# Sorted attention pairs: a two-row cluster code for the masks, a PSUM copy on ScalarE, and other points for ranks and masks

## The chip, the cores and the metric

The kernel runs on one core of a Trainium2 chip. The metric is the device time of one execution in microseconds (us); the time of a version is the median of several executions. Engines: PE (TensorE), DVE (VectorE), ACT (ScalarE), POOL (GpSimd) and SP (the queue that issues most DMAs). Each engine works through its own instructions in program order.

## The reference

Two parts, one after the other. First, routed attention for 4 batches x 8 heads, 768 tokens, head size 64: every query and every key goes to the nearest of its head's 16 centroids (argmax of the scores with the normalised centroids), and a query attends only to keys of its own cluster. Then a feed-forward layer on the 3072 x 512 result with the activation hardswish:

```python
mask = q_assign[:, :, :, None] == k_assign[:, :, None, :]
scores = np.where(mask, scale * np.matmul(q, k.transpose(0, 1, 3, 2)), -1e9)
x = softmax(scores) @ v               # (B, H, S, D) -> (B*S, H*D)
h = x @ w_in                          # 512 -> 2048
out = (h * np.clip(h + 3, 0, 6) / 6) @ w_out
```

## The kernel before, in words

Heads are worked on in 16 **pairs** of two heads. The first eight pairs take a dense way (768 x 768 scores with an additive mask, until about 250 us). The last eight, pairs 8 to 15, take a **sorted** way: queries and keys are sorted by cluster in DRAM, so that only a band of three 128-wide blocks around the diagonal has to be computed. All of the sorted work is issued by a loop of **rounds** g = 6 to 16, and a round has twelve **points**, 0 to 11 (`points`). A round works on three pairs at once: it computes the band of pair g (now), gets pair g+1 ready (next) and ranks pair g+2 (soon). Before the change the points are:

- 0 to 3: `band_scores` and `band_values` of pair g; point 0 also loads the natural rows of pair g+2 (`load_natural`)
- 4: `band_sums`, and `turn_back` of pair g-1
- 5: `band_divide` of pair g: transposes of the denominators and of the six numerator blocks on PE (L1047, L1051), then on DVE a reciprocal (L1055) and two multiplications that read the PSUM tile `ps` (L1058, tile `xr`); the result is stored by SP (L1064)
- 6: `gather` of pair g (twelve indirect DMAs on POOL), then `turn_natural` of pair g+2: twelve transposes on PE in two halves (L859: q, then k), each copied out by ACT (L860)
- 7: `cluster_scores` of pair g+2
- 8: `load_ranked` of pair g+1 and `load_rows` of pair g+2 (twelve DMAs on SP), then `own_clusters` of pair g+2: three transposes on PE (L878) and twelve small DVE operations in a row, from `mx` (L880) to the last `upto` (L889)
- 9: `order` of pair g+2: PE reads `upto` (L915, L928), DVE makes `edges` and `pos` (L929 to L940)
- 10: `scatter` of pair g+2: 24 indirect DMAs on POOL
- 11: `turn_ranked` and `band_masks` of pair g+1

After the work of each point the loop takes **one item of the feed-forward part** from a list (`fill`). A block of 256 tokens has 15 items: 8 **up items** (0 to 7), then 7 **down items** of which each is 16 matmuls. The items run straight through the rounds: round 6 begins with down item 1 of the first block, and each round takes twelve, so the item at point 5 of rounds 8 to 13 is down 0, up 5, up 2, down 6, down 3 and down 0. 51 items are left when the rounds end (785 us) and run alone.

An up item (`halved`) uses a seven-product scheme: 12 matmuls into PSUM tile `uX`, 16 into `uY`. DVE copies one of the uX blocks to SBUF (L652), adds twice (L645), and after uY adds three times; then ACT applies the ramp (`lift`, L499), and DVE finishes the *previous* item (`clip`, L502, and in every second item four `gated_sums`, L624, on DVE during the rounds). uX and uY, and X and Y of the down items, share a ring of two PSUM buffers (`psum_m`). The weights' sums `tx` come from DRAM: an item issues the load for the item two later (L548) on SP, into a ring of three.

`band_scores`, `turn_back`, `band_divide`, `turn_natural` and `turn_ranked` all take their PSUM tile `ps` from another ring of **two** (`psum_s`): every third user waits until the first one's tile has been read. `open_late` sets up the sorted part once, between the dense part and round 6; its first instruction on POOL is an iota into `places` (L795).

`band_masks` writes the additive mask of a pair as a product over cluster rows: two DVE operations for the query side (L974, L977) and two for the key side (L980, L981), each over 128 x 768.

Of the kernel before, what the change touches and what calls it, by code (L numbers as in the profile page):

```python
# [8 lines left out]
F32 = mybir.dt.float32  # L9
# [110 lines left out]
def fast_path(ctx, tc, ok, q, k, v, centroids, moe_w_in, moe_w_out, out):  # L120
# [457 lines left out]
    def ffn_items(b):  # L578
# [47 lines left out]
        def halved(b, m, u, i, g):  # L626
            token_sums(b, m)
            tx = st.pop(("tx", u))
            xb, xs = st["xb", b, m], st["xs", b, m]
            X = psum_m.tile([P, 4, P], F32, name="uX", tag="m")  # L630

            def part(dst, w, x):
                for kt in range(HK):
                    nc.tensor.matmul(  # L634
                        dst, lhsT=w[:, kt], rhs=x(kt), start=(kt == 0), stop=(kt == HK - 1)
                    )

            def a(s, r):
                return lambda kt: xb[:, s * HK + kt, r * P : (r + 1) * P]

            def s(k):
                return lambda kt: xs[:, k, kt]

            def add(out_, in0, in1):
                nc.vector.tensor_tensor(out=out_, in0=in0, in1=in1, op=ALU.add)  # L645


            part(X[:, 0], tx[:, 1], s(1))
            part(X[:, 1], wi(0, 0, i), a(0, 0))
            part(X[:, 2], wi(0, 1, i), a(0, 1))  # L650
            sx = sxp.tile([P, 4, P], F32, name="sx")
            nc.vector.tensor_copy(out=sx[:, 1], in_=X[:, 1])  # L652
            add(sx[:, 0], X[:, 0], sx[:, 1])
            add(sx[:, 2], X[:, 2], sx[:, 0])
            Y = psum_m.tile([P, 4, P], F32, name="uY", tag="m")
            part(Y[:, 0], tx[:, 0], s(0))
            part(Y[:, 1], wi(1, 0, i), a(1, 0))
            part(Y[:, 2], tx[:, 2], a(1, 1))
            part(Y[:, 3], wi(1, 1, i), s(2))
            add(sx[:, 3], Y[:, 0], sx[:, 0])  # L660
            add(g[:, 3], Y[:, 0], sx[:, 2])
            add(g[:, 0:3], Y[:, 1:4], sx[:, 1:4])
            lift(sx, g)
            finish()
            ending.append(lambda: (clip(g, sx, g), gated_sums(i)))
# [119 lines left out]
    def open_late():  # L785
        whole.close()
        late = ctx.enter_context(ExitStack())
        for name, bufs in (
            ("piecep", 2), ("svp", 1), ("fromp", 1), ("natp", 1), ("sortp", 1), ("bandp", 5),
            ("rowp", 3), ("rankp", 1), ("posp", 4),  # L790
        ):
            st[name] = right(late, name, bufs)
        rankp = st["rankp"]
        st["places"] = rankp.tile([P, S], mybir.dt.int16, name="places")
        nc.gpsimd.iota(  # L795
            st["places"], pattern=[[1, S]], base=0, channel_multiplier=0, allow_small_or_imprecise_dtypes=True
        )
        st["before"] = rankp.tile([P, P], BF16, name="before")
        nc.gpsimd.memset(st["before"], 0.0)
        nc.gpsimd.affine_select(  # L800
            out=st["before"], in_=st["before"], compare_op=ALU.is_ge, fill=1.0, base=0,
            pattern=[[-1, P]], channel_multiplier=1,
        )
        st["every"] = rankp.tile([P, P], BF16, name="every")
        nc.gpsimd.memset(st["every"], 1.0)
        st["runs"] = rankp.tile([P, 2, NCH, 2, C], BF16, name="runs")
        nc.gpsimd.memset(st["runs"], 0.0)
        st["steps"] = rankp.tile([P, 3, 2, 2, C // 2 + C], BF16, name="steps")
        nc.gpsimd.memset(st["steps"], 0.0)
        st["upto"] = rankp.tile([P, 2, C // 2 + 2 * D], BF16, name="upto")  # L810
        nc.gpsimd.memset(st["upto"], 0.0)
        least = st["least"] = smallp.tile([P, 1], F32, name="least")
        nc.vector.tensor_tensor(
            out=least, in0=ident[:, C - 1 : C], in1=ident[:, D + C - 1 : D + C], op=ALU.add
        )
        nc.vector.tensor_scalar(out=least, in0=least, scalar1=float(S), scalar2=None, op0=ALU.mult)
# [20 lines left out]
            load_piece((name + "nat", g), lambda t, x=x: natural(x, g, t))  # L837

    def load_rows(g):
        qn = st["qn", g] = st["fromp"].tile([P, NCH, 2, D], F32, name="qn")  # L840
        kvn = st["kvn", g] = st["fromp"].tile([P, NCH, 2, 2, D], F32, name="kvn")
        for t in range(2):
            nc.sync.dma_start(qn[:, :, t], natural(q, g, t))
        for t in range(2):
            for a, x in enumerate((k, v)):
                nc.sync.dma_start(kvn[:, :, t, a], natural(x, g, t))
# [25 lines left out]
    def own_clusters(g):  # L872
        st.pop(("xf", g))
        cs = st.pop(("cs", g))
        rankp = st["rankp"]
        pr = scratch([P, 2 * NC2, C], "pr")
        for i in range(NC2 // 4):
            nc.tensor.transpose(out=pr[:, 8 * i : 8 * i + 8], in_=cs[:, i], identity=ident)  # L878
        mx = rankp.tile([P, 2 * NC2], F32, name="mx")
        nc.vector.reduce_max(out=mx, in_=pr, axis=AX.X)  # L880
        oh = st["oh", g] = rankp.tile([P, 2, NCH, 2, C], BF16, name="oh")
        nc.vector.tensor_tensor(
            out=oh.rearrange("p a j t c -> p (a j t) c"), in0=pr,
            in1=mx.unsqueeze(2).to_broadcast([P, 2 * NC2, C]), op=ALU.is_ge,
        )
        runs, steps, upto = st["runs"], st["steps"], st["upto"]

        def add(out_, in0, in1):
            nc.vector.tensor_tensor(out=out_, in0=in0, in1=in1, op=ALU.add)  # L889

        nc.vector.tensor_copy(out=runs[:, :, 1], in_=oh[:, :, 0])
        for j in range(2, NCH):
            add(runs[:, :, j], runs[:, :, j - 1], oh[:, :, j - 1])
        w = C // 2
        own = steps[:, 0]
        add(own[:, :, :, w:], runs[:, :, NCH - 1], oh[:, :, NCH - 1])
        src = own
        for shift, dst in ((1, steps[:, 1]), (2, steps[:, 2]), (4, steps[:, 1]), (8, None)):
            to = summed(upto, 1) if dst is None else dst[:, :, :, w:]
            add(to, src[:, :, :, w:], src[:, :, :, w - shift : w + C - shift])  # L900
            src = dst

    def summed(upto, own):
        w = C // 2 - 1 + own
        return upto[:, :, w : w + 2 * D].rearrange("p a (t c) -> p a t c", t=2)[:, :, :, 0:C]

    def order(g):
# [12 lines left out]
        for a in range(2):  # L920
            dst = rk[:, a * half : (a + 1) * half].rearrange("p (j t c) -> p j t c", j=NCH, t=2)
            shape = [P, NCH, 2, C]
            for m, (lhsT, rhs) in enumerate((
                (st["before"], steps[:, 0, a, :, w:].unsqueeze(1).to_broadcast(shape)),
                (ident_q, runs[:, a]),
                (st["every"], summed(upto, 0)[:, a].unsqueeze(1).to_broadcast(shape)),
            )):
                nc.tensor.matmul(dst, lhsT=lhsT, rhs=rhs, start=(m == 0), stop=(m == 2))  # L928
        nc.vector.tensor_copy(  # L929
# [15 lines left out]
    def scatter(g):  # L945
        pos, qn, kvn = st["pos", g], st.pop(("qn", g)), st.pop(("kvn", g))
        done = {}
        for j in range(NCH):
            for t in range(2):
                for a, name in enumerate(("qd", "kvd")):  # L950
                    src = kvn[:, j, t].rearrange("p a d -> p (a d)") if a else qn[:, j, t]
# [17 lines left out]

    def band_masks(g):  # L970
        xm = st["xm", g] = st["sortp"].tile([P, NC2, P], BF16, name="xmsort")
        s, b = st["places"], edges[:, g - FIRST]
        xq, xk = (xm[:, a * NCH : (a + 1) * NCH].rearrange("p j c -> p (j c)") for a in range(2))
        nc.vector.tensor_scalar(  # L974
            out=xq, in0=s, scalar1=b[:, 0, 1:2], scalar2=-FAR, op0=ALU.is_lt, op1=ALU.mult
        )
        nc.vector.scalar_tensor_tensor(  # L977
            out=xq, in0=s, scalar=b[:, 0, 0:1], in1=xq, op0=ALU.is_ge, op1=ALU.mult
        )
        nc.vector.tensor_scalar(out=xk, in0=s, scalar1=b[:, 1, 0:1], scalar2=None, op0=ALU.is_lt)  # L980
        nc.vector.scalar_tensor_tensor(  # L981
            out=xk, in0=s, scalar=b[:, 1, 1:2], in1=xk, op0=ALU.is_ge, op1=ALU.max
        )

    def band(i):
        return max(i - 1, 0), min(i + 2, NCH)
# [93 lines left out]
    def points(g):  # L1080
# [8 lines left out]
            [lambda: now(band_values)(g, 0), lambda: now(band_scores)(g, 4, 5)],  # L1089
            [lambda: now(band_values)(g, 1)],  # L1090
            [lambda: now(band_sums)(g), lambda: past(turn_back)(g - 1)],
            [lambda: now(band_divide)(g)],
            [lambda: now(gather)(g), lambda: soon(turn_natural)(g + 2)],
            [lambda: soon(cluster_scores)(g + 2)],
            [lambda: next_(load_ranked)(g + 1), lambda: soon(load_rows)(g + 2), lambda: soon(own_clusters)(g + 2)],
            [lambda: soon(order)(g + 2)],
            [lambda: soon(scatter)(g + 2)],
            [lambda: next_(turn_ranked)(g + 1), lambda: next_(band_masks)(g + 1)],
        ]


# [487 lines left out]
```

## Time and profile before

| | |
|---|---|
| median of 3 runs | 993.72 us (993.04 to 994.1) |
| the profiled execution | 989.73 us, of which its span (first to last instruction) 987.9 us |
| PE busy | 941.9 us, 95% of the span |
| DVE, POOL, ACT busy | 631.4, 488.3 and 331.0 us |
| mean granted clock of PE | 0.988 |

The profiled execution is 1.83 us longer than its span. A row of the timeline reads: start in us from the span's start, duration in us, engine, line of the kernel, operation, what is written <- what is read, shape, number of merged instructions, and in brackets how long the engine had been idle before and what ended that. SPq is the issue of a DMA by SP. A row of the waits reads: engine, line, what it waited for, then total us, number of times, longest. The releaser is inferred, so a row can name the wrong one. In the windows view each row is a stretch of time with the busy us (and number of instructions) of PE, of PE's weight loads, of DVE, ACT and POOL, then the granted clock of PE, the share of the DMA engines that is busy and GB/s.

### The profile page before, as it was taken

To read this page: it belongs to the slowest core of one execution; us is meant where nothing else is said; L and a number is where in the kernel's file an instruction comes from. 1 tells how busy PE (TensorE), PEld (TensorE's weight loads), DVE (VectorE), ACT (ScalarE), POOL (GpSimd) and SP (SyncE) were. 2 spreads that over 40 slices of the span, in tenths; PEclk is the share of its full clock that TensorE was granted. 3 is DMA by queue.
4 is the path that set the end of the run, shared out by engine and by line. 5 is a ranking of instruction groups with operands and counts; after the bars stand their busy time and mean duration, and the time that the engine had idled before them with its cause. 6 is when DMAs were issued, how large, how long until landed. Compare 5 with 4: busy or idle time off the path is not lost. (4 is left out here: it accounts for less than half of the span.)

```text
span 987.9 us, 16752 instructions
## 1 busy us (share of the span) xinstructions
PE 941.9 (95%) x6358; PEld 734.2 (74%) x6358; DVE 631.4 (64%) x1399; ACT 331.0 (33%) x626; POOL 488.3 (49%) x438
## 2 busy tenths in 40 slices
PE   8999999999989999989979989999989989999997
PEld 5444445545888888777876877888888889999996
DVE  6889988989784773582583465575473482727270
ACT  6888876682111221322222122132322210202020
POOL 3877766767036456746376463674753040303030
PEclk9999999999999999999999989999999999999999
DMA  7245564321672936485491762858444242414120
GB/s 205 84 127 150 136 185 121 128 70 30 218 179 82 234 101 147 145 190 117 126 229 51 163 172 65 195 148 176 110 136 93 75 129 77 117 54 118 54 65 27
DMA packets 184587, 124.20 MB, mean 126 GB/s; under 512 B 146352, under 2 KB 162736, under 8 KB 184496
## 3 DMA queue, kind: packets, MB, share of 16 engines
q1 hardware_dynamic: 174560, 109.86, 42.8%
q0 software_dynamic: 9216, 12.60, 4.7%
q8 instruction: 53, 0.87, 0.4%
q10 hardware_dynamic: 720, 0.56, 0.2%
q14 instruction: 38, 0.31, 0.1%
HBM read 94.67 MB, written 28.31 MB: 124 GB/s over the span
## 5 line engine op out<-in xcount | busy, mean ns | idle before, releaser
L499 ACT ACTIVATE sx<-g_sb,half_c 128x512 f32<-128x512 f32 x88 | 63.6, 722 | 321.3 <-DVE g_sb L645 310.6
L965 POOL DMA_INDIRECT xn<-xsd,pos x96 | 94.8, 987 | 148.4 <-ACT sx L499 68.5
L433 POOL TENSOR_TENSOR acc<-acc,ex 128x768 f32<-128x768 f32 x64 | 123.3, 1927 | 34.6 <-ACT ex L423 31.1
L952 POOL DMA_INDIRECT qd<-qn,pos x96 | 97.9, 1020 | 76.5 <-DVE sx L645 29.0
L952 POOL DMA_INDIRECT kvd<-kvn,pos x96 | 96.4, 1004 | 34.3 <-issue 28.1
L624 POOL TENSOR_TENSOR g_sb<-g_sb 128x256 f32<-128x256 f32 x52 | 41.8, 824 | 137.3 <-DVE g_sb L502 136.3
L634 PE MATMUL uX<-xb,w_in_sb 128*128 128x128 f32 x704 | 95.2, 279 | 0.0
L669 PE MATMUL X<-w_out_sb,g_sb 128*128 128x256 f32 x384 | 91.5, 387 | 3.7 <-DVE sx L645 1.9
L669 PE MATMUL Y<-T,g_sb 128*128 128x256 f32 x384 | 87.4, 381 | 1.4 <-DVE rcp L473 1.4
L634 PEld LDWEIGHTS uX<-xb,w_in_sb 128*128 128x128 f32 x704 | 87.8, 196 | 0.0
L669 PE MATMUL Y<-w_out_sb,g_sb 128*128 128x256 f32 x384 | 87.3, 380 | 0.0
L676 DVE TENSOR_TENSOR y<-y,Y 128x256 f32<-128x256 f32 x48 | 20.2, 421 | 103.6 <-PE Y L669 102.7
L669 PEld LDWEIGHTS X<-w_out_sb,g_sb 128*128 128x128 f32 x384 | 72.0, 193 | 16.2 <-DVE g_sb L502 2.5
L669 PEld LDWEIGHTS Y<-T,g_sb 128*128 128x128 f32 x384 | 72.0, 190 | 13.6 <-issue 2.5
L669 PEld LDWEIGHTS Y<-w_out_sb,g_sb 128*128 128x128 f32 x384 | 72.1, 190 | 12.0 <-issue 2.7
L400 PE MATMUL ps<-xf 64*128 64x384 f32 x384 | 78.6, 487 | 0.6 <-ACT ex L423 0.6
L423 ACT ACTIVATE ex<-ps 128x768 f32<-128x768 f32 x96 | 72.5, 802 | 4.2 <-PE ps L400 4.2
L443 PE MATMUL pv<-ex,vt 128*64 128x384 f32 x384 | 72.5, 499 | 0.0
L634 PE MATMUL uX<-xs,tx 128*128 128x128 f32 x352 | 58.4, 289 | 11.5 <-DMA tx<-td 7.0
L634 PEld LDWEIGHTS uX<-xs,tx 128*128 128x128 f32 x352 | 46.8, 192 | 25.6 <-DVE g_sb L645 8.1
L645 DVE TENSOR_TENSOR g_sb<-uY,sx 128x128 f32<-128x128 f32 (+1 forms) x176 | 65.7, 415 | 0.0
L502 DVE SCALAR_TENSOR_TENSOR g_sb<-sx,g_sb 128x512 f32<-128x512 f32 x88 | 62.8, 717 | 2.0 <-ACT sx L499 2.0
(183 smaller groups left out, 1734.8 us busy)
## 6 DMA issues: line engine op xcount, KB each, us to landing
tx<-td SPq DMA_DIRECT2D x86, 384.0 KB
raw<-in_moe_w_in_dram SPq DMA_DIRECT2D x16, 512.0 KB
raw<-in_moe_w_out_dram SPq DMA_DIRECT2D x16, 512.0 KB
xb<-xd SPq DMA_DIRECT2D x12, 512.0 KB
out_dram<-y SPq DMA_DIRECT2D x44, 128.0 KB
qk<-in_q_dram SPq DMA_DIRECT2D x16, 192.0 KB
qk<-in_k_dram SPq DMA_DIRECT2D x16, 192.0 KB
vt<-in_v_dram SPq DMA_DIRECT2D x16, 192.0 KB
```

What stands on the lines that cost most here:

```text
L400: nc.tensor.matmul(st["ps", n][:, t, 0:HALF], lhsT=x[r, NCH + j], rhs=x[r, hf * NHC : (hf + 1) * NHC], start=first, stop=last, skip_group_ ...
L423: nc.scalar.activation(out=ex, in_=sc, func=ACT.Exp, scale=SM_SCALE)
L433: nc.gpsimd.tensor_tensor(out=acc, in0=acc, in1=ex, op=ALU.add)
L443: nc.tensor.matmul(pv[t * D : (t + 1) * D], lhsT=vt[:, t, j], rhs=ex[:, t], start=(j == 0), stop=(j == NCH - 1),)
L499: nc.scalar.activation(out=r, in_=h, func=ACT.Relu, bias=half_c, scale=1.0 / 6.0)
L502: nc.vector.scalar_tensor_tensor(out=g, in0=r, scalar=1.0, in1=h, op0=ALU.min, op1=ALU.mult)
L624: eng.tensor_tensor(out=out_, in0=in0, in1=in1, op=op)
L634: nc.tensor.matmul(dst, lhsT=w[:, kt], rhs=x(kt), start=(kt == 0), stop=(kt == HK - 1))
L645: nc.vector.tensor_tensor(out=out_, in0=in0, in1=in1, op=ALU.add)
L669: nc.tensor.matmul(bank[:, half * HC : (half + 1) * HC], lhsT=g_sb[:, kind, i], rhs=w[:, i], start=(first and i == 0), stop=(last and i == ...
L952: i = nc.gpsimd.indirect_dma_start(out=rows[name, g, t], in_=src, in_offset=None, out_offset=bass.IndirectOffsetOnAxis(ap=pos[:, a, j, t : ...
L965: nc.gpsimd.indirect_dma_start(out=xn[:, j, t], out_offset=None, in_=rows["xsd", g, t], in_offset=bass.IndirectOffsetOnAxis(ap=pos[:, 0, j ...
```

## The change

Five edits:

1. The copy of one uX block in the up items (L652) goes from DVE to ACT.
2. The mask code gets two rows per cluster, one for "at or behind the end of cluster c" and one, with positions and bounds negated, for "before it". With that a side needs one comparison in place of two operations. `open_late` gets three DVE instructions for it (`odd`, `sign`, and `places` multiplied by `sign` in place, which reads what POOL's iota wrote), `band_masks` one small one (`ends`); the last addition of `own_clusters` writes its sums into both rows.
3. `turn_natural` goes from point 6 to point 5, behind `band_divide`; `cluster_scores` from 7 to 6; `own_clusters` with `load_ranked` and `load_rows` from 8 to 7. `order` stays at point 9.
4. `band_masks` of pair g+1 goes from point 11 to point 8, between `own_clusters` and `order`.
5. The tile `qn` of `load_rows` is laid out by head first, so that its two loads write one contiguous run of 1536 bytes per partition in place of six of 256.

```diff
             sx = sxp.tile([P, 4, P], F32, name="sx")
-            nc.vector.tensor_copy(out=sx[:, 1], in_=X[:, 1])
+            nc.scalar.copy(out=sx[:, 1], in_=X[:, 1])
...
-        st["places"] = rankp.tile([P, S], mybir.dt.int16, name="places")
+        odd = st["odd"] = smallp.tile([P, 1], F32, name="odd")
+        nc.vector.tensor_reduce(
+            out=odd, in_=ident.rearrange("p (t r c) -> p r t c", t=2, c=C)[:, 1], axis=AX.XY, op=ALU.max
+        )
+        sign = st["sign"] = smallp.tile([P, 1], F32, name="sign")
+        nc.vector.tensor_scalar(out=sign, in0=odd, scalar1=-2.0, scalar2=1.0, op0=ALU.mult, op1=ALU.add)
+        places = st["places"] = rankp.tile([P, S], mybir.dt.int16, name="places")
         nc.gpsimd.iota(
...
+        nc.vector.tensor_scalar(out=places, in0=places, scalar1=sign, scalar2=None, op0=ALU.mult)
...
-        qn = st["qn", g] = st["fromp"].tile([P, NCH, 2, D], F32, name="qn")
+        qn = st["qn", g] = st["fromp"].tile([P, 2, NCH, D], F32, name="qn")
...
-            to = summed(upto, 1) if dst is None else dst[:, :, :, w:]
-            add(to, src[:, :, :, w:], src[:, :, :, w - shift : w + C - shift])
+            parts = [src[:, :, :, at : at + C] for at in (w, w - shift)]
+            to = dst[:, :, :, w:] if dst is not None else (
+                upto[:, :, w:].rearrange("p a (t r c) -> p a t r c", t=2, c=C)[:, :, :, 0:2]
+            )
+            if dst is None:
+                parts = [x.unsqueeze(3).to_broadcast([P, 2, 2, 2, C]) for x in parts]
+            add(to, *parts)
...
     def band_masks(g):
         xm = st["xm", g] = st["sortp"].tile([P, NC2, P], BF16, name="xmsort")
+        ends = st["rankp"].tile([P, 2], F32, name="ends")
+        nc.vector.tensor_scalar(
+            out=ends, in0=edges[:, g - FIRST, :, 1], scalar1=st["sign"], scalar2=st["odd"],
+            op0=ALU.mult, op1=ALU.add,
+        )
...
-            out=xq, in0=s, scalar1=b[:, 0, 1:2], scalar2=-FAR, op0=ALU.is_lt, op1=ALU.mult
-        nc.vector.scalar_tensor_tensor(
-            out=xq, in0=s, scalar=b[:, 0, 0:1], in1=xq, op0=ALU.is_ge, op1=ALU.mult
-        nc.vector.tensor_scalar(out=xk, in0=s, scalar1=b[:, 1, 0:1], scalar2=None, op0=ALU.is_lt)
-        nc.vector.scalar_tensor_tensor(
-            out=xk, in0=s, scalar=b[:, 1, 1:2], in1=xk, op0=ALU.is_ge, op1=ALU.max
+            out=xq, in0=st["places"], scalar1=ends[:, 0:1], scalar2=-FAR, op0=ALU.is_ge, op1=ALU.mult
+        nc.vector.tensor_scalar(out=xk, in0=st["places"], scalar1=ends[:, 1:2], scalar2=None, op0=ALU.is_lt)
...
-            [lambda: now(band_divide)(g)],
-            [lambda: now(gather)(g), lambda: soon(turn_natural)(g + 2)],
-            [lambda: soon(cluster_scores)(g + 2)],
-            [lambda: next_(load_ranked)(g + 1), lambda: soon(load_rows)(g + 2), lambda: soon(own_clusters)(g + 2)],
+            [lambda: now(band_divide)(g), lambda: soon(turn_natural)(g + 2)],
+            [lambda: now(gather)(g), lambda: soon(cluster_scores)(g + 2)],
+            [lambda: soon(own_clusters)(g + 2), lambda: next_(load_ranked)(g + 1), lambda: soon(load_rows)(g + 2)],
+            [lambda: next_(band_masks)(g + 1)],
             [lambda: soon(order)(g + 2)],
             [lambda: soon(scatter)(g + 2)],
-            [lambda: next_(turn_ranked)(g + 1), lambda: next_(band_masks)(g + 1)],
+            [lambda: next_(turn_ranked)(g + 1)],
```

More of the change, by code (lines that the diff above doesn't have):

```diff
@@ L793, in open_late @@
         rankp = st["rankp"]
-        st["places"] = rankp.tile([P, S], mybir.dt.int16, name="places")
+        odd = st["odd"] = smallp.tile([P, 1], F32, name="odd")
[5 more added lines that the diff above has]
+        places = st["places"] = rankp.tile([P, S], mybir.dt.int16, name="places")
         nc.gpsimd.iota(
-            st["places"], pattern=[[1, S]], base=0, channel_multiplier=0, allow_small_or_imprecise_dtypes=True
+            places, pattern=[[1, S]], base=0, channel_multiplier=0, allow_small_or_imprecise_dtypes=True
         )
+        nc.vector.tensor_scalar(out=places, in0=places, scalar1=sign, scalar2=None, op0=ALU.mult)
         st["before"] = rankp.tile([P, P], BF16, name="before")
@@ L839, in load_rows @@
     def load_rows(g):
-        qn = st["qn", g] = st["fromp"].tile([P, NCH, 2, D], F32, name="qn")
+        qn = st["qn", g] = st["fromp"].tile([P, 2, NCH, D], F32, name="qn")
         kvn = st["kvn", g] = st["fromp"].tile([P, NCH, 2, 2, D], F32, name="kvn")
         for t in range(2):
-            nc.sync.dma_start(qn[:, :, t], natural(q, g, t))
+            nc.sync.dma_start(qn[:, t], natural(q, g, t))
         for t in range(2):
@@ L898, in own_clusters, with summed @@
         for shift, dst in ((1, steps[:, 1]), (2, steps[:, 2]), (4, steps[:, 1]), (8, None)):
-            to = summed(upto, 1) if dst is None else dst[:, :, :, w:]
-            add(to, src[:, :, :, w:], src[:, :, :, w - shift : w + C - shift])
+            parts = [src[:, :, :, at : at + C] for at in (w, w - shift)]
[5 more added lines that the diff above has]
+            add(to, *parts)
             src = dst
-    def summed(upto, own):
-        w = C // 2 - 1 + own
+    def summed(upto):
+        w = C // 2 - 1
         return upto[:, :, w : w + 2 * D].rearrange("p a (t c) -> p a t c", t=2)[:, :, :, 0:C]
@@ L925, in order @@
                 (ident_q, runs[:, a]),
-                (st["every"], summed(upto, 0)[:, a].unsqueeze(1).to_broadcast(shape)),
+                (st["every"], summed(upto)[:, a].unsqueeze(1).to_broadcast(shape)),
             )):
@@ L950, in scatter @@
                 for a, name in enumerate(("qd", "kvd")):
-                    src = kvn[:, j, t].rearrange("p a d -> p (a d)") if a else qn[:, j, t]
+                    src = kvn[:, j, t].rearrange("p a d -> p (a d)") if a else qn[:, t, j]
                     i = nc.gpsimd.indirect_dma_start(
@@ L971, in band_masks @@
         xm = st["xm", g] = st["sortp"].tile([P, NC2, P], BF16, name="xmsort")
-        s, b = st["places"], edges[:, g - FIRST]
+        ends = st["rankp"].tile([P, 2], F32, name="ends")
[3 more added lines that the diff above has]
+        )
         xq, xk = (xm[:, a * NCH : (a + 1) * NCH].rearrange("p j c -> p (j c)") for a in range(2))
         nc.vector.tensor_scalar(
-            out=xq, in0=s, scalar1=b[:, 0, 1:2], scalar2=-FAR, op0=ALU.is_lt, op1=ALU.mult
+            out=xq, in0=st["places"], scalar1=ends[:, 0:1], scalar2=-FAR, op0=ALU.is_ge, op1=ALU.mult
         )
-        nc.vector.scalar_tensor_tensor(
-            out=xq, in0=s, scalar=b[:, 0, 0:1], in1=xq, op0=ALU.is_ge, op1=ALU.mult
-        )
-        nc.vector.tensor_scalar(out=xk, in0=s, scalar1=b[:, 1, 0:1], scalar2=None, op0=ALU.is_lt)
-        nc.vector.scalar_tensor_tensor(
-            out=xk, in0=s, scalar=b[:, 1, 1:2], in1=xk, op0=ALU.is_ge, op1=ALU.max
-        )
+        nc.vector.tensor_scalar(out=xk, in0=st["places"], scalar1=ends[:, 1:2], scalar2=None, op0=ALU.is_lt)
     def band(i):
```

## The prediction

> **What bounds the kernel now.** I read the page first, then the waits of PE, then the timeline around each long wait, last the granted clock in windows.
>
> ```profile
> PE 941.9 (95%) x6358; PEld 734.2 (74%) x6358; DVE 631.4 (64%) x1399; ACT 331.0 (33%) x626; POOL 488.3 (49%) x438
> ```
> PE is the bound. Whatever DVE, ACT or SP save counts only where PE waits for them. So these are the rows to change:
>
> ```profile
> PE rk L915 <- DVE upto L889: 10.3, 5, 3.7
> PE uX L634 <- DMA tx<-td: 7.0, 4, 2.9
> PE uX L634 <- DVE sx L645: 4.2, 5, 1.2
> PE ps L996 <- DVE xmsort L981: 3.8, 2, 2.2
> PE X L669 <- DVE sx L645: 1.9, 2, 0.9
> PE ps L859 <- PE ps L859: 0.8, 2, 0.4
> ```
> The windows view shows a second price, in its column PEclk; the first and the last of four such stretches:
>
> ```profile
> 280.80:284.20 3.40, 3.40 (x19) 3.40 (x18) 3.26 (x10) 0.71 (x1) 0.00 (x0) 0.50 0.00 0
> 574.30:581.10 6.80, 6.12 (x29) 6.16 (x30) 0.88 (x3) 0.00 (x0) 5.28 (x6) 0.50 0.22 74
> ```
> The waits add up to 28.0 us. In the four stretches (3.4, 6.8, 3.4 and 6.8 us, at 281, 441, 568 and 574) PE has half its clock: 20.4 us, and less the waiting inside them about 9.4 us of lost work (an estimate). What the moved points touch first is `order` waiting for `upto` (10.3) and the band waiting for its mask (3.8).
>
> **Part 1, setup: a new wait on DVE.** `places` is now multiplied on DVE right after POOL's iota.
>
> ```profile
> 251.47 0.15 DVE L813 TENSOR_TENSOR least<-ident 128x1 f32<-128x1 f32 x1
> 251.62 0.42 SPq L477 DMA_DIRECT2D xd<-num  x1
> 253.32 0.41 DVE L676 TENSOR_TENSOR y<-y,X 128x256 f32<-128x256 f32 x1
> 254.74 0.77 POOL L795 IOTA places<- 128x768 int16 x1 [8.89 <-DVE tx L556]
> 254.80 3.62 PE L669 MATMUL X<-w_out_sb,g_sb 128*128 128x256 f32 x16
> ```
> The iota starts only at 254.74; its releaser is named as a DVE operation that comes later in the program, so it was another: the store of `num` issued at 251.62, whose memory is reused. DVE reached this place at about 251.5 (L813 stands just behind it). Now it stands until the iota ends (255.5), multiplies (0.42, the price of L974 below) and is some 4.5 us late with all that is queued behind: the `tx` sums and the addition at 253.32 that frees X. X starts at 254.80 and had 1.07 us of slack (253.73 to 254.80). PE loses 4.5 - 1.07 = **+3.5 us**, once (0 if the iota came early, 4.5 at most). Two further small instructions are inside that.
>
> **Part 2, `turn_natural` behind `band_divide`.** Both take `ps` from the ring of two: the k half of `turn_natural` needs the buffer that DVE reads in L1058. So far one item stood between. In round 8:
>
> ```profile
> 364.79 0.82 PE L1051 MATMUL ps<-ident,bn 128*128 128x128 f32 x6
> 365.45 1.89 PE L669 MATMUL X<-w_out_sb,g_sb 128*128 128x256 f32 x8
> 369.00 1.02 DVE L1058 TENSOR_TENSOR xr<-ps,inverses 128x384 f32<-128x384 f32 x2
> 370.12 0.85 PE L859 MATMUL ps<-ident,piece 128*128 128x128 f32 x6 [0.40 <-PE ps L859]
> ```
> The k half starts 0.1 us after L1058 ends at 370.02, even behind an item of 3.5 us: the ring shows. With the item moved behind it, the q half runs 365.45 to 366.1 (0.66, six transposes like L1051's) and PE then stands until 370.05: 3.9 where it was 0.4. What hid this wait was the item. The other rounds, by the end of L1051's block (its start plus 0.65) and of L1058:
>
> ```profile
> 421.74 0.82 PE L1051 MATMUL ps<-ident,bn 128*128 128x128 f32 x6
> 424.98 1.02 DVE L1058 TENSOR_TENSOR xr<-ps,inverses 128x384 f32<-128x384 f32 x2
> ...
> 484.93 0.82 PE L1051 MATMUL ps<-ident,bn 128*128 128x128 f32 x6
> 486.59 1.02 DVE L1058 TENSOR_TENSOR xr<-ps,inverses 128x384 f32<-128x384 f32 x2
> ...
> 549.24 1.02 DVE L1058 TENSOR_TENSOR xr<-ps,inverses 128x384 f32<-128x384 f32 x2 [0.42 <-PE ps L1051]
> ...
> 671.79 0.82 PE L1051 MATMUL ps<-ident,bn 128*128 128x128 f32 x6
> 675.99 1.02 DVE L1058 TENSOR_TENSOR xr<-ps,inverses 128x384 f32<-128x384 f32 x2
> ```
> Round 9: 426.05 - 423.05 = 3.0. Round 10: 1.4. Round 11, where DVE was idle and L1058 followed L1051 at once: 0.6; round 12, also with a down item ahead, the same. Round 13: 3.9. Together 13.4, less 0.8 that is there already: **+12.6 us**. Rounds 8 and 13 come at the end of the up items, where DVE still owes two `clip`s and four `gated_sums`; behind them stand only down items, which have no slack to give back.
>
> **Part 3, masks and copy.**
>
> ```profile
> L974 DVE TENSOR_SCALAR xmsort<-places,edges 128x768 bf16<-128x768 int16 x8 | 3.4, 420 | 0.0
> L977 DVE SCALAR_TENSOR_TENSOR xmsort<-places,edges,xmsort 128x768 bf16<-128x768 int16 x8 | 8.2, 1019 | 0.3
> L652 DVE COPY sx<-uX 128x128 f32<-128x128 f32 x88 | 25.4, 289 | 41.4 <-PE uX L634 38.9 <-DVE g_sb L502 0.5
> L710 ACT COPY y<-X 128x256 f32<-128x256 f32 x12 | 4.5, 371 | 53.0 <-PE X L669 50.3 <-DMA xsd<-xr 2.7
> ```
> A pair's masks cost DVE 2 x (0.42 + 1.02) = 2.9 us, and then 2 x 0.42 and about 0.2 for `ends`: 1.0 (the side of L980 and L981 costs the same). Made three points earlier they are ready before the band: **-3.8 us**. The copy on ACT is not in the trace; it lies between 0.2 and 0.37 (L710, twice as wide), I take 0.28, as on DVE. Behind it on ACT stands `lift`, which waits for DVE anyway; ACT is busy a third. It helps where DVE runs behind PE; the chain then loses about 0.23 us in every second up item. That is about four waits outside the sorting points (rounds 14 and 15): **-0.9 us** (0 to -2).
>
> **Part 4, `own_clusters`, one item, then `order`.** Does the 10.3 go? In rounds 7, 8, 12 and 13 down items stand there and nothing was waited for. In rounds 6, 9, 10 and 11 up items do, and DVE has a backlog:
>
> ```profile
> 500.51 0.55 DVE L880 TENSOR_REDUCE mx<-pr 128x24 f32<-128x384 f32 x1
> 503.71 0.19 DVE L889 TENSOR_TENSOR upto<-steps 128x64 bf16<-128x64 bf16 x1
> 503.96 0.25 PE L915 MATMUL rk<-every,upto 128*128 128x1 bf16 x4 [3.09 <-DVE upto L889]
> ...
> 557.10 0.98 SPq L833 DMA_DIRECT2D piece<-qd  x2
> 568.47 12.31 SPq L548 DMA_DIRECT2D tx<-td  x4
> 574.98 1.19 PE L634 MATMUL uX<-xs,tx 128*128 128x128 f32 x4 [2.88 <-DMA tx<-td]
> ...
> 837.28 1.82 PE uY L634 x16
> ...
> L645 DVE TENSOR_TENSOR sx<-uX,sx 128x128 f32<-128x128 f32 x176 | 51.3, 292 | 6.0
> L645 DVE TENSOR_TENSOR g_sb<-uY,sx 128x384 f32<-128x384 f32 x88 | 48.2, 548 | 0.0
> L502 DVE SCALAR_TENSOR_TENSOR g_sb<-sx,g_sb 128x512 f32<-128x512 f32 x88 | 62.8, 717 | 2.0 <-ACT sx L499 2.0
> L624 DVE TENSOR_TENSOR g_sb<-g_sb 128x256 f32<-128x256 f32 x140 | 53.4, 423 | 2.4
> ```
> The chain of `own_clusters` takes 3.4 us (500.51 to 503.9). Now the next item's additions stand behind it, and PE's next uX needs the buffer they free. So `upto` is ready in time and `sx` is late instead. Followed through by these durations (PE 28 matmuls of 0.113, 3.16 us, per up item; on DVE 0.6 for the first two additions, about 1.0 for the next three, 0.65 for `clip` and 1.6 for four `gated_sums`, each a little under the rows' sum as they overlap):
> - round 6: waits of 4.2 (1.7 of it at `order`) become 1.3 + 1.5 + 0.7: -0.7
> - round 9: 3.7 becomes 3.5, at down 0, whose X needs the buffer of the last uX: -0.2
> - round 10: 3.1 + 0.2 + 1.6 (`tx`) become 1.9 + 1.3 + 0.3: -1.4
> - round 11: 1.6 + 0.2 + 2.9 (`tx`) become 1.3 and a longer `tx` wait: the twelve loads of point 8 occupy SP from 557.10 to 568.4, and the `tx` behind them landed 17.9 us after they began. Issued a point earlier, behind the same stores, they begin at about 556 and are about 2 us shorter in all, as two contiguous `qn` loads are cheaper (edit 5; an estimate, 0 to 3). The first `tx` behind them, now one item earlier, lands at about 572; PE wants it at 567: 5 us. +1.6
>
> Sum **-0.7 us**; the ends are -17.5 (all of these waits gone) and +6 (the loads find the scatter unfinished in rounds 9 to 11). I stay near the worked rows. In round 12 the shorter loads end a `tx` wait: **-1.2**.
>
> **Part 5, the clock.** Half speed follows waits: 1.72 and 3.71 us (rounds 6 and 9), 1.57 and 2.88 (round 11), but not 3.09 (round 10). The changed kernel has some eight waits over 1.5 us as now, but six of them are 3 us or longer, where there are two or three. At 2 us for each long and 0.8 for a short one: 13.6 against 9.4, less where a wait falls beside another; I take **+2.5 us** (-4 to +6).
>
> The Trainium skill (TensorE: Matmul & The Clock Gate, Part 1) has the clock halved after at least one idle window of 3.4 us. The trace disagrees, with half speed after 1.72 us and full speed after 3.09. By that rule the term would be larger (rival C).
>
> **Sum:** 3.5 + 12.6 - 3.8 - 0.9 - 0.7 - 1.2 + 2.5 = **+12.0 us**. The profiled execution would take 989.7 + 12.0 = 1001.7; added to the median, which lies 4 us higher, 993.7 + 12.0 = **1005.7**.
>
> **Rivals.**
> - **A, faster:** nothing takes the place of the waits at `order`: part 4 gives -17.5 and the clock -9.4. Then 993.7 + 16.1 - 3.8 - 1.2 - 0.9 - 17.5 - 9.4 = 977, or 986 if the new waits of parts 1 and 2 cost as much clock as the old ones. For it: the 10.3 us row. Against: DVE has no free time in those items. Chance 0.13.
> - **B, no change:** the ring's wait costs half (DVE's `xr` comes earlier, or the waiting of PE lets DVE work off its backlog in rounds 9 and 10): 1005.7 - 6.3 - 4 for the clock = 995. Against: in rounds 8 and 13 DVE's chain hangs on uY's end alone. Chance 0.12.
> - **C, slower still:** each of the five waits over 3.4 us (setup, rounds 8, 9, 11, 13) costs 6.8 us at half speed, as after the 3.71: 3.4 lost each, 17 against 9.4, so +5 over the forecast, 1011; a late scatter that holds SP comes on top, 1015. Chance 0.15.
> - Forecast 1000 to 1009: 0.60.
>
> The range 991 to 1014 leaves out most of A and the end of C. A measurement can tell about 0.2% (2 us) from no change. Faster by over that 0.15, within 0.07, slower 0.78.
>
> **What would show it.** Right: PE L859 waiting about 3.9, 3.0, 1.4, 0.6, 0.6 and 3.9 us in rounds 8 to 13, ending just after L1058; a DVE gap of 3.6 us ended by POOL's iota and PE's X late by 3.5; no wait of L915 or of the band for masks; new waits of uX for `sx` or `tx` in rounds 6, 9, 10, 11. Wrong: L859 without waits (part 2 falls, and with it the sign), or the rows of L915 gone with no `sx` or `tx` row grown (A).

## The result, and the profile after

The kernel before took 993.23 us (median of 15 runs, 989.92 to 997.28), the changed one 996.62 us (15 runs, 994.1 to 1002.14): ratio 1.0041, 95% interval [1.0025, 1.0057]. It is slower by about 4 us, where 12.0 were predicted. The profiled run of after took 996.47 us (span 994.6), that of before 989.73, which is 3.5 under its own median; so the two traces differ by 6.7 us of span, more than the medians do.

The page of after, part 1: DVE and POOL have less to do, ACT more, PE as much as before.

```profile
span 994.6 us, 16794 instructions
PE 941.7 (95%) x6358; PEld 734.1 (74%) x6358; DVE 594.4 (60%) x1306; ACT 351.2 (35%) x714; POOL 486.4 (49%) x438
```

PE's waits in after (engine, tile and line waited for: us in total, times, longest):

```profile
PE uX L634 <- issue: 9.2, 7, 2.3
PE uX L634 <- DMA tx<-td: 9.1, 3, 5.2
PE X L669 <- DVE sx L645: 5.2, 3, 3.7
PE X L669 <- DVE y L676: 4.2, 1, 4.2
PE ps L866 <- ACT xnat L867: 3.6, 4, 0.9
PE ps L866 <- PE ps L866: 1.0, 2, 0.5
```

The rows for `upto` (10.3) and for the mask (3.8) are gone, as intended. In their place stand waits of uX and X for `sx` ("issue" is what the profile prints where it can't name the releaser), longer ones for `tx`, the setup wait and, for the k half, a row for the copy `xnat` (the last row is the k half as well). Laid side by side by place, PE's idle time before and after: setup 0 and 4.2 us; round 6 3.8 and 4.4; the last item of round 7, for `tx`, 0 and 1.1; the k half 0.8 and 4.6; round 9 3.7 both; round 10 4.7 and 2.7; round 11 4.5 and 6.8; round 12 1.2 and 2.8; the band's mask 3.8 and 0; rounds 14 and 15 5.3 and 5.1. That is +7.6; idle times too short to be listed here and PE's busy time are 0.9 lower, which leaves the 6.7. (The prediction has 4.2, 4.9 and 4.7 for rounds 6, 10 and 11 of before; PE's idle times in its trace add up to the 3.8, 4.7 and 4.5 given here.) The clock stood at half for 20.5 us in both, and PE was busy for 19.0 us of that in both.

The setup in after, from the timeline (start, duration, what, and in brackets the idle time before it and its releaser):

```profile
251.51 0.42 SPq L477 DMA_DIRECT2D xd<-num  x1
255.49 0.77 POOL L801 IOTA places<- 128x768 int16 x1 [9.75 <-DMA piece<-in_q_dram]
256.29 0.42 DVE L804 TENSOR_SCALAR places<-places,sign 128x768 int16<-128x768 int16 x1 [4.56 <-POOL places L801]
258.56 0.41 DVE L676 TENSOR_TENSOR y<-y,X 128x256 f32<-128x256 f32 x1
259.03 5.41 PE L669 MATMUL X<-w_out_sb,g_sb 128*128 128x256 f32 x16 [4.18 <-DVE y L676]
```

DVE stands 4.56 us for POOL, its addition L676 is late, and PE's X waits 4.18. The last row shows a second price: the 16 matmuls take 5.41 us where the same X took 3.62 before.

Round 8 of after, where the prediction counted 3.9 us:

```profile
370.43 0.82 PE L1061 MATMUL ps<-ident,bn 128*128 128x128 f32 x6
371.09 0.82 PE L866 MATMUL ps<-ident,piece 128*128 128x128 f32 x6
371.99 0.78 ACT L867 COPY xnat<-ps 128x768 f32<-128x768 f32 x1
372.82 0.87 PE L866 MATMUL ps<-ident,piece 128*128 128x128 f32 x6 [0.91 <-ACT xnat L867]
374.64 1.02 DVE L1068 TENSOR_TENSOR xr<-ps,inverses 128x384 f32<-128x384 f32 x2
```

The k half (372.82) starts when the ACT copy of the q half ends (371.99 + 0.78), and long before DVE has read `band_divide`'s buffer (374.64 to 375.66). So it doesn't use that buffer. DVE itself is as late as the prediction had it: it reads until 375.66, 3.9 us after the end of the q half (371.75).

### The profile page after: what moved, and what is told of

Read it like the earlier page. It is cut to its first block, busy times and chain, and to the rows that moved or that the text cites. A ratio compares the mean times of both kernels' runs of the same rounds, so it can differ in the third digit from the quotient of the medians.

```text
span 994.6 us, 16794 instructions
## 1 busy us (share of the span) xinstructions
PE 941.7 (95%) x6358; PEld 734.1 (74%) x6358; DVE 594.4 (60%) x1306; ACT 351.2 (35%) x714; POOL 486.4 (49%) x438
## 4 chain that ended last, share of the span: by engine, by line
PE 66%; DVE 4%; DMA 3%; issue 1%; ACT 1%; SPq 1%; POOL 0%; POOLq 0%; ACTq 0%
PE Y L669 16%; PE uY L634 15%; PE X L669 13%; PE uX L634 12%; PE ps L1006 4%; PE pv L1023 3%; PE ps L866 2%; DMA tx<-td 2%; DVE g_sb L645 1%; PE pd L1044 1%; DVE g_sb L624 1%; DVE sx L645 1%; DMA xn<-xsd,pos 1%; PE pcs L337 1%; DVE tx L556 0%
## 5 line engine op out<-in xcount | busy, mean ns | idle before, releaser
L669 PE MATMUL X<-w_out_sb,g_sb 128*128 128x256 f32 x384 | 93.9, 394 | 11.2 <-DVE sx L645 5.2
L676 DVE TENSOR_TENSOR y<-y,Y 128x256 f32<-128x256 f32 x48 | 20.2, 421 | 130.4 <-PE Y L669 129.6
L645 DVE TENSOR_TENSOR sx<-uX,sx 128x128 f32<-128x128 f32 x176 | 51.1, 290 | 73.1 <-ACT sx L652 69.7
```

Of the source, the lines that this page charges most:

```text
L669: nc.tensor.matmul(bank[:, half * HC : (half + 1) * HC], lhsT=g_sb[:, kind, i], rhs=w[:, i], start=(first and i == 0), stop=(last and i == ...
```

## The experiments

All ratios are to the kernel before, run beside it on the same chip; where edits are undone or redone, line numbers shift by a few. Summary first (median in us, ratio, PE's idle time in waits over 0.3 us and its time at half clock, both between 250 and 900 us of one trace):

| kernel | median | ratio | idle in waits | half clock |
|---|---|---|---|---|
| before | 993.2 | 1 | 27.5 | 20.5 |
| after | 996.6 | 1.0041 | 35.4 | 20.5 |
| late_sign | 990.4 | 0.9978 | 28.9 | 13.7 |
| old_points | 991.7 | 0.9989 | 31.9 | 17.1 |
| old_points_late_sign | 986.1 | 0.9938 | 27.4 | 13.7 |
| points_only | 997.2 | 1.0045 | 35.7 | 23.9 |
| copy_only | 991.4 | 0.9991 | 32.0 | 13.7 |
| masks_only | 990.4 | 0.9971 | 28.0 | 20.5 |
| qn_only | 991.4 | 0.9988 | 28.2 | 17.1 |
| k_after_xr | 1012.2 | 1.0195 | 43.4 | 34.1 |
| loads_late | 990.4 | 0.9977 | 31.1 | 13.7 |
| split_turn | 983.2 | 0.9898 | 24.4 | 10.2 |

**late_sign** is after with the multiplication out of the setup.

```diff
-        nc.vector.tensor_scalar(out=places, in0=places, scalar1=sign, scalar2=None, op0=ALU.mult)
...
     def band_masks(g):
         xm = st["xm", g] = st["sortp"].tile([P, NC2, P], BF16, name="xmsort")
+        if g == FIRST:
+            nc.vector.tensor_scalar(
+                out=st["places"], in0=st["places"], scalar1=st["sign"], scalar2=None, op0=ALU.mult
+            )
```

> The changed kernel with the multiplication of places by sign taken out of the setup and put in front of the first band_masks (round 7), long after the iota. Theory S (the wait of DVE for the iota is a real loss): the 4.6 us gap of DVE at 252 us and PE's 4.2 us wait for y (L676) go, and the half-speed stretch behind it (260.1 to 263.5, 1.7 us lost) with them: 4 to 6 us faster than the changed kernel, ratio to the kernel before 0.998 to 1.000. Rival (the wait is taken out of slack that the rounds have anyway, or only the phase of the clock differs): within 1.5 us of the changed kernel, ratio 1.0025 to 1.0055.

0.9978 [0.9961, 0.9995]. The setup wait cost about 6 us (1.0041 to 0.9978), more than its 4.2 us of waiting: the half clock behind it goes too.

```profile
255.36 0.77 POOL L801 IOTA places<- 128x768 int16 x1 [8.88 <-DVE tx L556]
255.43 3.62 PE L669 MATMUL X<-w_out_sb,g_sb 128*128 128x256 f32 x16
```

The iota comes as late as in after; nobody waits for it, and X takes 3.62 us again.

**old_points** is after with the points of before (edits 3 and 4 undone); **old_points_late_sign** has the edit of late_sign as well.

```diff
-            [lambda: now(band_divide)(g), lambda: soon(turn_natural)(g + 2)],
-            [lambda: now(gather)(g), lambda: soon(cluster_scores)(g + 2)],
+            [lambda: now(band_divide)(g)],
+            [lambda: now(gather)(g), lambda: soon(turn_natural)(g + 2)],
...
```

> The changed kernel with the twelve points of the kernel before (edits 3 and 4 undone; copy, mask code and qn layout stay). Theory P (the move of the points gains nothing: it trades the waits at order for waits on sx, tx and the k half): order waits for upto again, about 9 us in all, the masks' wait shrinks from 3.8 to about 1, the k half waits 0.8 in place of 4.6, tx about 6 in place of 9: 2 to 5 us faster than the changed kernel, ratio to the kernel before 0.998 to 1.002. Rival (the moved points are a gain that the setup hides): the waits at order and the band come back without anything in exchange, 3 to 8 us slower than the changed kernel, ratio 1.007 to 1.012.

> The changed kernel with all points as before (edits 3 and 4 undone) and the multiplication of `places` moved from the setup into the first `band_masks`: so the cheap masks, the copy on ScalarE and the `qn` layout alone, without the setup wait. Theory: the setup wait (4.3 us in the run with the points of before, and 1.7 us of half clock behind it) goes and nothing takes its place; from 991.7 about 986, ratio to before 0.992 to 0.995, and no PE row for y L676. Rival: the time saved is spent again at `order`, which waits for `upto` on a DVE with the same backlog: the `upto` waits grow from 10.6 us and the ratio stays at 0.997 to 0.999.

old_points 0.9989 [0.9969, 1.0008]; old_points_late_sign 0.9938 [0.9915, 0.9961]: 5 us for the setup, as in late_sign within the intervals. And against late_sign, 0.9938 to 0.9978: the new points cost 4 us, as they do on the kernel before:

**points_only** is before with edits 3 and 4 alone (the hunk of `points` in the change's diff), **masks_only** with edit 2 (those of `open_late`, `summed` and `band_masks`, with the multiplication as in late_sign), **copy_only** and **qn_only** with one line or three:

```diff
-            nc.vector.tensor_copy(out=sx[:, 1], in_=X[:, 1])
+            nc.scalar.copy(out=sx[:, 1], in_=X[:, 1])
```

```diff
-        qn = st["qn", g] = st["fromp"].tile([P, NCH, 2, D], F32, name="qn")
+        qn = st["qn", g] = st["fromp"].tile([P, 2, NCH, D], F32, name="qn")
...
-            nc.sync.dma_start(qn[:, :, t], natural(q, g, t))
+            nc.sync.dma_start(qn[:, t], natural(q, g, t))
```

> The kernel before with edits 3 and 4 alone (the new points, with the old masks and the copy on DVE). Theory P: k half +3.8, tx +2 to +4 (no shorter loads here), band's wait for masks -3.8, the waits at order replaced by sx waits that are longer than in the changed kernel, as DVE has 1.9 us more per pair for masks and the copies to do: 1 to 5 us slower than before, ratio 1.001 to 1.005. Rival (the moved points are a gain): 3 to 8 us faster, ratio 0.992 to 0.997.

> The kernel before with edit 1 alone (the uX copy on ScalarE). Theory: 0.23 us less in each second up item where DVE runs behind, some 7 waits, and the same off DVE's backlog before order: 1 to 3 us faster, ratio 0.997 to 0.999. Rival (the handover from ACT costs more than the copy on DVE did): DVE waits for the copy in the items, ratio 1.000 to 1.003.

> The kernel before with edit 2 alone (masks in the two-row code), and the multiplication of `places` in the first `band_masks`, so without the setup wait. Theory: the masks carry most of the 6.7 us that the copy, the masks and the `qn` layout gave together with the points of before: the band's waits for its mask (3.8 us) shrink to 1 or go, and with them at most one half clock stretch (1.7): 3.5 to 5.5 us, ratio 0.994 to 0.997, about 988 to 989. Rival: the masks alone give under 2 us (ratio 0.998 to 1.000), and the gain needs the copy beside them.

> The kernel before with edit 5 alone (the `qn` tile with t ahead of j, so that each load writes a contiguous run per partition). Theory of the prediction (the loads at point 8 get shorter by up to 3 us, the `tx` waits of rounds 11 and 12 fall by 1 to 3 us): ratio 0.997 to 0.999. Rival: the loads are as long as before, or the `tx` comes no earlier: ratio 0.999 to 1.001 and `tx` waits of 7 us as before.

points_only 1.0045 [1.0023, 1.0066]: the moves by themselves are slower, by what the whole change is. copy_only 0.9991 [0.9973, 1.0009] and qn_only 0.9988 [0.9971, 1.0004]: each lies about 1 us under before, and neither can be told from no change. masks_only 0.9971 [0.9952, 0.9991]: 2.8 us, short of the 3.5 to 5.5 expected. The three together gave 6.2 (old_points_late_sign). qn_only's `tx` waits fell to 3.5 us from 7.0, but its waits for `sx` rose from 4.2 to 5.9 and nothing measurable was left.

**k_after_xr** tests the failed step directly. One instruction makes the k half of after wait for `xr`, as the prediction had it:

```diff
-        turn_piece(st.pop(("knat", g)), xf[:, NCH:])
+        piece, xr = st.pop(("knat", g)), st.pop("divided", None)
+        if xr is not None:
+            one = piece[:, 0, 0, 0:1]
+            nc.vector.scalar_tensor_tensor(
+                out=one, in0=xr[:, NCH - 1, 1, 0:1], scalar=0.0, in1=one, op0=ALU.mult, op1=ALU.add
+            )
+        turn_piece(piece, xf[:, NCH:])
...
+        xr = st["divided"] = st["rowp"].tile([P, NCH, 2, D], F32, name="xr", tag="row")
```

> The changed kernel, with the k half of `turn_natural` made to wait for `band_divide`'s `xr` by one added instruction on DVE (one number of the k piece, plus zero times the last number of `xr`): the wait that the prediction counted on. Theory (only the buffer was wrong, the price was right): the k half waits about 3.9, 3.0, 1.4, 0.6, 0.6 and 3.9 us in rounds 8 to 13 in place of 4.6 us in all, +8 to +10 us: 1003 to 1006, ratio to before 1.011 to 1.015. Rival (DVE works its backlog off while PE stands, so that the later waits for `sx` and `tx` shrink by about half of it): 999 to 1001, ratio 1.006 to 1.009.

1012.24 us, 1.0195 [1.0171, 1.0219]: 15.6 us over after. Rounds 8 and 9, from the timeline (L1074 is `xr`, L875 the added instruction):

```profile
372.26 0.82 PE L866 MATMUL ps<-ident,piece 128*128 128x128 f32 x6
375.81 1.02 DVE L1074 TENSOR_TENSOR xr<-ps,inverses 128x384 f32<-128x384 f32 x2
376.87 0.16 DVE L875 SCALAR_TENSOR_TENSOR piece<-xr,piece 128x1 f32<-128x1 f32 x1
377.13 0.85 PE L866 MATMUL ps<-ident,piece 128*128 128x128 f32 x6 [4.05 <-issue]
...
438.22 0.85 PE L866 MATMUL ps<-ident,piece 128*128 128x128 f32 x6 [3.09 <-issue]
```

The waits are 4.05, 3.09, 1.50, 0.70, 0.70 and 4.03 us; predicted were 3.9, 3.0, 1.4, 0.6, 0.6 and 3.9. So the working of that part was right to 0.15 us, about as long as the added instruction takes (0.16), for a kernel that wasn't built. Neither theory had the whole price: the k half's waits grow by 9.4 us over after, all waits together by 8.0 (so the others shrink by a seventh of it, not by the half of the rival), and half clock from 20.5 to 34.1 us, in which PE is busy 32.1 instead of 19.0: another 6.5. Together that is 14.5 of the 15.8 us by which the spans differ.

**split_turn** takes the k half's wait away: late_sign with the q half a point earlier, so that an item stands between the halves (`turn_keys` is the k half, cut off `turn_natural`).

```diff
-            [lambda: now(band_sums)(g), lambda: past(turn_back)(g - 1)],
-            [lambda: now(band_divide)(g), lambda: soon(turn_natural)(g + 2)],
+            [lambda: now(band_sums)(g), lambda: past(turn_back)(g - 1), lambda: soon(turn_natural)(g + 2)],
+            [lambda: now(band_divide)(g), lambda: soon(turn_keys)(g + 2)],
```

> The kernel without the setup wait (places multiplied in the first `band_masks`), with the q half of `turn_natural` a point earlier (4) and the k half left in point 5 behind `band_divide`. Theory: an item then stands between the two halves, the k half finds its buffer copied, and the six waits of 0.5 to 0.9 us (4.6 us) go: from 990.4 to about 986 to 987, ratio to before 0.993 to 0.996. Rival: these waits are only the room in which DVE catches up; in the up items the next waits for `sx` grow by the same, and the ratio stays at 0.997 to 0.999.

983.22 us, 0.9898 [0.9877, 0.9918], faster than both kernels and by more than expected. Round 8 (L865 at 360.74 is the q half, at 365.56 the k half):

```profile
360.74 0.87 PE L865 MATMUL ps<-ident,piece 128*128 128x128 f32 x6
362.38 0.80 ACT L866 COPY xnat<-ps 128x768 f32<-128x768 f32 x1
364.91 0.82 PE L1066 MATMUL ps<-ident,bn 128*128 128x128 f32 x6
365.56 0.82 PE L865 MATMUL ps<-ident,piece 128*128 128x128 f32 x6
369.12 1.02 DVE L1073 TENSOR_TENSOR xr<-ps,inverses 128x384 f32<-128x384 f32 x2
```

The six waits (4.6 us) are gone. In round 9 the wait of X for `sx` (3.7) is gone as well, and a `tx` wait of 2.5 stands there; in round 10 a wait of 1.5 stands where one of 0.4 stood. All waits together are 4.5 us shorter, and one window of half clock less (PE busy at half clock 9.5 us instead of 12.7) gives 1.6. That is 6.1 of the 8.2 us by which the spans differ; where the rest comes from was not traced. With the halves apart the points earn 4 us (0.9938 to 0.9898); as the change made them they cost 4.

**loads_late** is late_sign with `load_ranked` and `load_rows` back at point 8.

```diff
-            [lambda: soon(own_clusters)(g + 2), lambda: next_(load_ranked)(g + 1), lambda: soon(load_rows)(g + 2)],
-            [lambda: next_(band_masks)(g + 1)],
+            [lambda: soon(own_clusters)(g + 2)],
+            [lambda: next_(load_ranked)(g + 1), lambda: soon(load_rows)(g + 2), lambda: next_(band_masks)(g + 1)],
```

> The kernel without the setup wait, with `load_ranked` and `load_rows` back at point 8 (own_clusters stays at 7, the masks at 8). Theory of the prediction's part 4 (loads a point earlier make the next `tx` of round 11 late for its item): the `tx` waits fall from 6.1 us to 3 or 4 and the ratio to before from 0.998 to 0.995 to 0.996. Rival: the `tx` waits are set by how many loads stand in SP's queue, not by the point (the run with the copy alone has the loads at point 8 and 9.0 us of them): 6 to 9 us as it is, ratio 0.997 to 1.000.

0.9977 [0.9962, 0.9992], as late_sign; the rival held. SP's rows in round 11 say why:

```profile
558.97 0.98 SPq L839 DMA_DIRECT2D piece<-qd  x2
560.04 2.69 SPq L839 DMA_DIRECT2D piece<-kvd  x2
...
568.40 1.59 SPq L852 DMA_DIRECT2D kvn<-in_v_dram  x1
570.09 3.37 SPq L548 DMA_DIRECT2D tx<-td  x3
```

The twelve loads still hold SP for 11 us with the `tx` loads behind them. They begin 4.0 us later than in late_sign (558.97 against 554.98), so PE meets the late `tx` one item later and waits 4.4 us where it waited 4.6. **split_loads** was to part them: split_turn with `load_rows` at point 3; split_loads_again and loads_beside are the same kernel, turn_beside is split_turn.

```diff
-            [lambda: now(band_values)(g, 1)],
+            [lambda: now(band_values)(g, 1), lambda: soon(load_rows)(g + 2)],
...
-            [lambda: soon(own_clusters)(g + 2), lambda: next_(load_ranked)(g + 1), lambda: soon(load_rows)(g + 2)],
+            [lambda: soon(own_clusters)(g + 2), lambda: next_(load_ranked)(g + 1)],
```

> The kernel with the halves of `turn_natural` in points 4 and 5 (983.2 us, ratio to before 0.990, `tx` waits 10.7 us), with the six loads of `load_rows` four points earlier (3 instead of 7), so that six and not twelve loads stand together in SP's queue. Theory (in round 11 the `tx` is late because twelve loads hold SP's queue from 549.9 to 561.0 us): that wait falls from 5.0 us by about the 5.3 us that `load_rows` takes there, the half clock behind it goes too, in all 4 to 6 us less: 977 to 980, ratio to before 0.984 to 0.987. Rival (the loads hold up another `tx` at point 3, or wait there for the scatter to free their buffer and hold SP for longer): 983 to 987, ratio 0.990 to 0.994, `tx` waits of 9 us or more at other places.

> The same kernel as in the run with `load_rows` at point 3, whose chip took 1212.5 us for the kernel before too, so that its waits can't be set beside the others. Where the kernel before takes about 993: theory 977 to 980 us, ratio to before 0.984 to 0.987, with the `tx` wait of round 11 gone from 5.0 us to under 1; rival 983 to 987, ratio 0.990 to 0.994, with `tx` waits of 9 us or more at other places.

> The kernel with the halves of `turn_natural` in points 4 and 5 once more, beside the next one. Where the kernel before takes about 993: ratio 0.988 to 0.992 as measured, `tx` waits of 10.7 us, 5.0 of them in round 11.

> The same with `load_rows` at point 3. Theory (twelve loads together in SP's queue make the `tx` of round 11 late): 4 to 6 us below the kernel beside it, ratio to before 0.984 to 0.987, that wait under 1 us. Rival (the loads hold another `tx` up): within 2 us of the kernel beside it, or above it.

These four runs came on chips where the kernel before too takes 1212 to 1217 us, with `tx` waits and others everywhere; only the ratios say something: 0.9891 [0.9852, 0.9931], 0.9898 [0.9859, 0.9937], and side by side 0.9882 [0.9830, 0.9935] for split_turn against 0.9889 [0.9845, 0.9934] with the loads parted. split_turn gains about as much there; whether parted loads shorten the wait of round 11 where before takes 993 stays open.

## Why the prediction was wrong

The direction was right and the time lies in the range, but the size was about three times too large. That the sign held owes something to luck: the prediction itself hung it on the long waits of the k half, and these did not come; what made up for a good part of them are `tx` waits that part 4 had put too low. The time is near that of rival B (995), but B's reason, a DVE that gets to `xr` sooner or works its backlog off, is not what the traces show.

- **Part 2 is the step that failed**: "the k half of `turn_natural` needs the buffer that DVE reads in L1058". I read "a ring of two" as strict turns: `band_divide`, q, k, hence the first buffer again for k. In the kernel before, the program as built does take turns (`band_divide` bank 0, the q half 2, the k half 0 in each of rounds 8 to 13), so its trace was read rightly. But in the changed kernel as built, both halves have the same buffer in rounds 8, 9, 10 and 13 (by the addresses in its list of instructions: in round 8 `band_divide` writes PSUM bank 0, the q half bank 2 and the k half bank 2 again), and the k half's wait names ACT, where before it named DVE. Only in rounds 11 and 12 does k take `band_divide`'s buffer, and there the wait came out as priced (0.5, predicted 0.6). In the other four it became that for one ACT copy, 0.91; in all 3.8 us more than before instead of 12.6. Why the scheduler of the program chose so is not in the trace. k_after_xr shows that the wait I priced had the right size, and split_turn that even the small one is worth removing.
- **Part 1** was right in its place and its wait (4.2, predicted 3.5). With the half clock behind it, for which part 5 had the term, late_sign and old_points_late_sign put it at 5 to 6 us.
- **Part 3**: the band's two waits for its mask went as predicted (-3.8). Alone the masks gave 2.8 us; the copy took 0.26 us on ACT (0.28 predicted), and its gain can't be told from none.
- **Part 4**: the substitution was right. `upto` is ready and `sx` is late instead: round 6 4.4 (predicted 3.5), round 9 3.7 (3.5), round 10 2.7 (3.5), round 11 1.5 and 5.2 (1.3 and 5). Rival A, for whom nothing takes the place of these waits, had no case. Round 12 had the wrong sign: the `tx` wait grew from 1.2 to 2.8 where I let it end, and at the end of round 7 one of 1.1 came that I hadn't counted. The loads didn't get shorter by 2 us in round 11 either: they held SP for 11.3 us, before for 11.4. With all this the part came to +3.6 instead of -1.9.
- **Part 5**: +2.5 predicted, 0 in the trace: of the six waits of 3 us or longer that it counted, three came (the setup, rounds 9 and 11) and the three of the k half did not. Where those came too (k_after_xr) the clock took 6.5 us more than in after, so for its own premise the term was too small.

In the trace, then: 8.8 us too much for the k half and 2.5 for the clock, against 5.5 too little in part 4 and 0.7 each in part 1 and for the copy: from 12.0 to the 7.6 of the places listed above.

## What to carry to other kernels

A pool of two buffers under a scheduler is not a ring: look in the built program for which buffer each tile got and what its wait names, before pricing a wait by turns. Here, work moved ahead of a wait on a loaded engine only traded the place of the wait (`upto` for `sx`), whereas an item put between two users of one buffer removed it: with `turn_natural` split over two points the kernel was 8 us faster than with both halves behind `band_divide` (split_turn against late_sign). When a wait is priced, ask how much of it falls into one window of the clock, below.

## What was not expected of the hardware

The half clock of PE follows a fixed grid. In each of twelve traces every half-clock stretch starts a whole number of 3.413 us after the others (after: 260.12, 444.44, 509.30, 577.56 and 744.82; the differences are 54, 19, 20 and 49 windows), and each is one or two windows long. What goes with it is how long PE is busy inside one window. Windows laid on that grid (columns: window, its length, busy time with counts of PE, PEld, DVE, ACT, POOL, then PEclk); after, around the setup wait:

```profile
253.29:256.71 3.42, 1.56 (x8) 1.03 (x6) 0.42 (x2) 0.00 (x0) 1.14 (x3) 1.00 1.00 228
256.71:260.12 3.41, 1.09 (x5) 0.99 (x6) 3.24 (x11) 0.00 (x0) 1.20 (x5) 1.00 0.44 148
260.12:263.53 3.41, 3.41 (x10) 2.66 (x9) 3.27 (x10) 0.00 (x0) 0.00 (x0) 0.50 0.41 157
```

The 4.2 us wait lies across two windows; the one with 1.09 us busy is followed by half clock, the one with 1.56 is not. copy_only and before, both around round 9's wait of 3.7 us:

```profile
437.85:441.26 3.41, 1.50 (x7) 0.97 (x6) 3.20 (x10) 0.00 (x0) 2.50 (x4) 1.00 1.22 272
441.26:444.68 3.42, 1.62 (x15) 1.52 (x16) 2.26 (x11) 0.00 (x0) 1.58 (x2) 1.00 1.31 218
444.68:448.09 3.41, 3.41 (x18) 3.00 (x17) 0.93 (x3) 0.37 (x1) 0.13 (x1) 1.00 1.22 211
```

```profile
437.81:441.22 3.41, 0.49 (x3) 0.09 (x1) 3.14 (x12) 0.00 (x0) 2.50 (x4) 1.00 1.32 228
441.22:444.63 3.41, 2.62 (x14) 2.29 (x15) 1.90 (x8) 0.00 (x0) 2.79 (x3) 0.50 1.33 218
499.24:502.65 3.41, 1.63 (x15) 1.44 (x13) 3.17 (x11) 0.00 (x0) 2.50 (x4) 1.00 1.33 219
502.65:506.06 3.41, 2.04 (x21) 1.81 (x22) 3.17 (x13) 0.35 (x1) 2.80 (x3) 1.00 1.32 217
```

In copy_only the grid cuts the wait in half (1.50 and 1.62 us busy) and the clock stays; in before 2.9 us of it fall into one window (0.49) and the next is at half. The last two rows are the 3.09 us wait of round 10, also cut in two, behind which the prediction found full clock. The 1.72 us wait of round 6 lies in one window:

```profile
277.38:280.79 3.41, 1.70 (x18) 1.46 (x19) 3.00 (x14) 0.00 (x1) 0.00 (x0) 1.00 0.62 194
```

Its 1.70 us busy were followed by half clock, though the 1.50 to 1.63 us above were not, so in this band the busy time alone does not decide. Counted over the windows at full clock between 245 and 790 us in the twelve traces: with under 1.40 us busy, all 44 were followed by half clock; from 1.40 to 1.79, 7 of 25; above, none of some 1760. At half clock, windows with 2.84 us busy or more went back to full, those with 2.77 or less did not. So a wait of 2.0 us inside one window costs another 1.7, and one of 3.7 across two may cost nothing; which it is depends on where the grid lies, and part of the spread of the runs (990 to 997 us for before) may come from that, which wasn't tried.

The Trainium skill (TensorE: Matmul & The Clock Gate, Part 1) states a free-running window of 3413 ns, and the traces agree to the digit. It has the clock halved after at least one idle window; here all 44 windows with up to 1.38 us of work (40% busy) sufficed.
